# Decode attention and gated MLP on one core: output weights in 4 KB rows, down products that write output rows, and keys taken with step eight

## The chip, the cores and the metric

The kernel runs on one core of one Trainium2 chip. Its engines work in parallel, each on its own stream of instructions: PE (TensorE, matrix products, with weight loads listed apart as PEld), DVE (VectorE), ACT (ScalarE), POOL (GpSimd) and SP (SyncE), which here only issues DMAs. 16 DMA engines move data between memory and the core's SBUF. The metric is the device time of one execution in microseconds (us); less is better.

## The reference

One token for each of 4 sequences passes through a pre-norm attention block with a cache, and then a gated MLP. Inputs are bfloat16: 32 heads of 128, 8192 cached keys per head, width 512, hidden width 1792.

```python
def _A_ref(x, k_cache, v_cache, wq, wo):
    B, Sq, D = x.shape
    H, Dh = 32, 128
    q = (lambda x, *d: x.transpose(*d))((x @ wq).reshape(B, Sq, H, Dh), 0, 2, 1, 3)
    scores = jnp.einsum("bhqd,bhkd->bhqk", q, k_cache) * (Dh ** -0.5)
    p = _softmax(scores, axis=-1)
    o = jnp.einsum("bhqk,bhkd->bhqd", p, v_cache)
    return (lambda x, *d: x.transpose(*d))(o, 0, 2, 1, 3).reshape(B, Sq, H * Dh) @ wo

def _B_ref(x, w_gate, w_up, w_down):
    g = jnp.einsum("bsd,df->bsf", x, w_gate)
    u = jnp.einsum("bsd,df->bsf", x, w_up)
    h = _sigmoid(g) * u
    return jnp.einsum("bsf,fd->bsd", h, w_down)

x = A_x
h = x + _A_ref(_layernorm(x, axis=-1), A_k_cache, A_v_cache, A_wq, A_wo)
h2 = h + _B_ref(_layernorm(h, axis=-1), B_w_gate, B_w_up, B_w_down)
```

The two caches hold 256 MiB each, so nearly all of the traffic is cache. wq and wo have 4 MiB each, gate, up and down 1.75 MiB each.

## The kernel before, in words

**Pairs and slots.** The unit of work is a pair: two heads of one sequence, 4 MiB of K or of V. There are 64 K pairs and 64 V pairs. A pair fills one of four slots of `KV`: the 128 partitions are 2 heads x 64, and each partition holds 128 consecutive keys of 128 numbers, so one partition is one run of 32 KB in memory. Four pairs (the four sequences of two heads) form a group; there are 16 groups.

**Queue.** All loads are issued by SP in a fixed order (`order`, from L320): wq; K pairs 0 and 1; wo; then K and V pairs alternating, with K four pairs ahead of V; at the end the weights gate, up and down, which use slots too. Each load waits on SP until its slot is free: after the last transpose of a K pair (L367) or after the last PV product of a V pair (L458). What stands behind a waiting load on SP waits as well. K pair 0 comes in four loads, V pair 63 in two, down in three pieces (8, 4 and 2 of the 14 blocks of 128 hidden rows); every other load is one DMA. wo takes the place of wq in `Wreg`, so its load (L318) waits for the q projection (L511).

**Scores.** A K pair is worked through in 8 chunks of 16 keys per partition. DVE transposes a chunk in 32x32 blocks of 32-bit words (L367) from the slot into `kTc`, and PE multiplies it with four shifted windows of q (L386), adding the rows of all chunks and pairs of a group in one PSUM bank. Before the change, chunk s is the run of keys 16s to 16s+15 of every partition.

**Softmax.** At the end of a group come a maximum (L398, L403, L407, L411, L416), the exponential into `E_sb` (L421), the sums (L427, L429), a scaling (L430) and two transposes into `PT` (L439). These steps are spread over the following ticks, a tick being one chunk of K or V.

**PV.** Chunk m of a V pair is four products with 32 stationary columns each, which run side by side on PE (L458); their 512 moving columns are four keys that lie 16 apart.

**Selection and projection.** At the end of a group ACT copies the sums to `O_sb` (L486). Two ticks later four float32 products with `O_sb` as the stationary side pick the wanted diagonal parts and turn them (L494), DVE casts the eight columns to `OT` (L499), and two ticks after that 8 products with wo (L476) and an addition into `sth` (L481) follow. In `sth`, width lies across the partitions: column 4b+c holds block c of sequence b.

**End.** After the last group: layer norm (L205 to L223), gate and up products with the weights stationary (L582), sigmoid on ACT (L587), its product with up into `hhT` (L589), 56 down products with w_down stationary and 4 moving columns (L597) in three parts that wait for the three pieces, addition of `sth` (L602), a product that turns the result into 16 rows (L604), a cast (L606) and the store (L607).

Of the kernel before, what the change touches and what calls it, by code (L numbers as in the profile page):

```python
# [5 lines left out]
BF16 = mybir.dt.bfloat16  # L6
FP32 = mybir.dt.float32
# [8 lines left out]
GH = 8  # L16
# [63 lines left out]
def bass_sequential_preLN__mha_block_cached__glu_gated_glu__decode_kernel(  # L80
# [32 lines left out]
    with ExitStack() as es:  # L113
        def SB(name, shape, dt):
            return es.enter_context(nc.sbuf_tensor(name, shape, dt))
# [13 lines left out]
        xnT = SB("xnT", [128, NDC * B], BF16)  # L129
        hnT = SB("hnT", [128, NDC * B], BF16)  # L130
        q_all = SB("q_all", [128, NH], BF16)
        selrep = SB("selrep", [128, 4, 128], BF16)
        amask = SB("amask", [128, 4], BF16)
        q2 = SB("q2", [128, 4, NH], BF16)
        Lq = SB("Lq", [128, NLQ, 4, W], BF16)
        KV = SB("KV", [128, NSL, R * 128], BF16)
        kTc = SB("kTc", [128, NKT, RC * 64], FP32)
        E_sb = SB("E_sb", [128, 512], BF16)
        PT = SB("PT", [128, 2, PTW], BF16)
        mpart = SB("mpart", [128, 1], FP32)  # L140
        mrow = SB("mrow", [1, GH], FP32)
# [1 line left out]
        sig = SB("sig", [128, 1], FP32)  # L143
        rsum = SB("rsum", [128, 1], FP32)
        O_sb = SB("O_sb", [128, 512], FP32)
        OT = SB("OT", [128, 2, GH], BF16)
        sg_sb = SB("sg_sb", [128, NFT * B], FP32)
        hhT = SB("hhT", [128, NFT * B], BF16)
        h2T = SB("h2T", [128, NDC * B], BF16)
        o_sb = SB("o_sb", [NDC * B, 128], BF16)  # L150
        dummy = SB("dumm", [128, 2], FP32)
        WREG = H * D
        Wreg = SB("Wreg", [128, WREG], BF16)
        wq_v = Wreg[:, :].rearrange("p (c f) -> p c f", c=NDC)
        wo_v = Wreg[:, :].rearrange("p (h f) -> p h f", h=H)

        def raw(t):
            return t.tensor if hasattr(t, "tensor") else t
# [19 lines left out]
        keys += [f"sl{i}" for i in range(NSL)] + [f"k0p{i}" for i in range(4)] + [f"vl{i}" for i in range(2)]  # L178
        for k in keys:
            prog.sems[k] = es.enter_context(nc.semaphore("s_" + k))  # L180

# [45 lines left out]
        def f_xT(e):  # L227
# [19 lines left out]
            bass.AP(raw(M8), 0, [[GH, 128], [GP, 2], [0, 16], [1, GP]])), [t_m8])  # L247


        t_am = emit("dve", lambda e: e.tensor_reduce(  # L250
            amask[:, :], identf[:, :].rearrange("p (a j) -> p a j", a=4), AX.X, ALU.max), [t_identf])
        for c in range(2):
# [61 lines left out]
        t_qproj = []  # L314

        def emit_wo():
            src = A_wo.rearrange("(h p) f -> p h f", p=128)
            t_wo.append(prog.dma("sp", "wo", lambda e: e.dma_start(wo_v[:, :, :], src), [t_qproj[0]]))  # L318

        steps = [("k", n) for n in range(LAGP)]  # L320
        for n in range(NP):
# [13 lines left out]
        def pump():  # L335
            while next_dma[0] < len(order) and ready(*order[next_dma[0]]):
                kind, n = order[next_dma[0]]
                next_dma[0] += 1
                if kind == "k":
                    emit_pair("k", n, A_k_cache, t_k, "k0p", 4 if n == 0 else 1)  # L340
                elif kind == "v":
                    emit_pair("v", n, A_v_cache, t_v, "vl", 2 if n == NP - 1 else 1)
                elif kind == "wq":
                    emit_wq()
                elif kind == "wo":
                    emit_wo()
                else:
                    emit_weight(kind)
# [7 lines left out]
        t_oev = {}  # L356
        t_ptc = {}
        t_pvg = {}
        st_ = dict(xs=t_xst, xo=None, lq=None, h=t_h, ot=[None, None])
        t_lq = {}  # L360

        KVW = KV[:, :, :].bitcast(FP32)

        def transposes(n, s):
            u = NCH * n + s
            slot = slot_of["k", n]
            t_copy[u] = emit("dve", lambda e: e.transpose(  # L367
                kTc[:, u % NKT, :], KVW[:, slot, 64 * RC * s:64 * RC * (s + 1)]), [t_k[n][s * len(t_k[n]) // NCH], t_score.get(u - NKT)])
            if s == NCH - 1:
                t_tr[n] = t_copy[u]  # L370

# [70 lines left out]
        def pv(u):  # L442
            n, m = u // NCH, u % NCH
            g, i = n // GP, n % GP
            first = i == 0 and m == 0
            last = i == GP - 1 and m == NCH - 1
            slot = slot_of["v", n]
            half = m // 4
            w = [t_v[n][half * len(t_v[n]) // 2], t_ptc[g]]
            if first and g > 1:  # L450
                w.append(t_oev[g - 2])

            def f(e):
                mms = []
                for j in range(4):
                    rr = 4 * (m % 4) + j
                    o = (2 * rr + half) * 128 + i * 32
                    mms.append(e.matmul(obank(g)[32 * j:32 * (j + 1), :], PT[:, g % 2, o:o + 32],  # L458
                                        in_slot(slot, [[RC * 128, 4], [1, 128]], (64 * half + rr) * 128),
                                        start=first, stop=last, tile_position=(0, 32 * j)))  # L460
                return mms if last else mms[-1]
            tok = emit("pe", f, w, incs=4 if last else 1)
            if m == NCH - 1:
                t_pv[n] = tok
            if last:
                t_pvg[g] = tok

        def project(g, t_ot):
            ob = g % 2

            def f(e):
                ins = None
                for c in range(NDC):
                    for hh in range(2):
                        h = 2 * g + hh
                        ins = e.matmul(cols(bank[XO][:, 64:64 + NDC * B], c), wo_v[:, h, 128 * c:128 * (c + 1)],  # L476
                                       OT[:, ob, B * hh:B * (hh + 1)], start=(hh == 0), stop=(hh == 1))
                return ins
            t = emit("pe", f, [t_ot, *t_wo])
            st_["ot"][ob] = t  # L480
            st_["h"] = st_["xo"] = emit("dve", lambda e: e.tensor_tensor(  # L481
                sth[:, 0:NDC * B], sth[:, 0:NDC * B], bank[XO][:, 64:64 + NDC * B], ALU.add), [t, st_["h"]])

        def finish(g):
            ob = g % 2
            t_oev[g] = emit("act", lambda e: e.activation(O_sb[:, :], obank(g), ACT.Copy),  # L486
                            [t_pvg[g], st_.get("sel")])
            box = {}
# [100 lines left out]
        t_hh = emit("dve", lambda e: e.tensor_tensor(hhT[:, :], sg_sb[:, :], bank[UBK][:, 0:NF], ALU.mult), [t_sg, t_u])  # L589

        wd_v, t_wd = t_w["wd"]
        for i in range(len(WDT) - 1):
            def f_down(e, i=i):
                ins = None
                for t in range(WDT[i], WDT[i + 1]):
                    for c in range(NDC):
                        ins = e.matmul(cols(bank[DBK], c), wd_v[:, t, 128 * c:128 * (c + 1)],  # L597
                                       hhT[:, B * t:B * (t + 1)], start=(t == 0 and c == 0),
                                       stop=(t == NFT - 1), skip_group_check=True)
                return ins  # L600
            t_d = emit("pe", f_down, [t_hh, t_wd[i]])
        t_h2 = emit("dve", lambda e: e.tensor_tensor(  # L602
            h2T[:, :], sth[:, 0:NDC * B], bank[DBK][:, 0:NDC * B], ALU.add), [t_d, st_["h"]])
        t_o = emit("pe", lambda e: e.matmul(bank[XS][0:NDC * B, 0:128], h2T[:, :], ident[:, :],  # L604
                                            start=True, stop=True), [t_h2])
        t_oc = emit("dve", lambda e: e.tensor_copy(o_sb[:, :], bank[XS][0:NDC * B, 0:128]), [t_o])  # L606
# [58 lines left out]
```

## Time and profile before

| | |
|---|---|
| median of 3 runs | 1295.3 us (1295.19 to 1295.32) |
| profiled execution, its own time | 1295.28 us |
| its span | 1293.4 us |
| PE busy | 800.3 us (62%) |
| DVE busy | 720.8 us (56%), of which the transposes L367 587.7 us, x512 |
| ACT, POOL busy | 28.0 us, 10.3 us |
| moved by DMA | 551.45 MB, mean 426 GB/s over the span |

The span is what the profiler records between the first and the last instruction; 1.88 us of the execution's time lie outside it. Busy shares are means over the whole span. The profile also cuts the span into 40 slices of 32.3 us, and gives the busy tenths of each engine and the rate of the DMAs for each. "The chain" is found by going back from the last instruction to what released it, and so on to the start. In the listing of DMA issues, the time to landing counts from the issue on SP, so it includes the wait behind earlier loads of the same queue.

### The profile page before, as it was taken

What the parts mean: (1) busy time and instruction counts of PE and PEld (TensorE: products, weight loads), DVE (VectorE), ACT (ScalarE), POOL (GpSimd) and SP (SyncE); (2) the same over time, 40 slices, a digit from 0 to 9 for tenths busy, and PEclk for the clock granted to TensorE, in tenths of its full rate; (3) what the DMA queues carried; (4) which work ended last, traced back from release to release, by engine and by line L of the source; (5) the groups of instructions that cost most, each with busy time, mean ns of one, the idle gap of its engine ahead of it and who ended that gap; (6) DMA issues with size and microseconds to landing.
All of it is one profiled execution on the core that took longest, in us unless ns stands there. A gap on an engine that the chain in (4) does not pass through costs nothing.

```text
span 1293.4 us, 10558 instructions
## 1 busy us (share of the span) xinstructions
PE 800.3 (62%) x4761; PEld 318.5 (25%) x4761; DVE 720.8 (56%) x766; ACT 28.0 (2%) x56; POOL 10.3 (1%) x11
## 2 busy tenths in 40 slices
PE   4576556647558566566656667576575666566464
PEld 2122222213223122222222223122222222222122
DVE  5585655637555455545647556465555646556340
ACT  0000000000000000000000000000000000000001
POOL 3000000000000000000000000000000000000000
PEclk9698788777787787787786887787887887877775
DMA  9999999999999999999999999999999999999997
GB/s 394 408 429 435 427 433 432 427 434 430 430 431 430 433 429 432 429 433 429 429 436 429 429 433 427 435 428 430 435 426 434 428 433 434 424 435 431 428 432 306
DMA packets 26244, 551.45 MB, mean 426 GB/s; under 512 B 2260, under 2 KB 8152, under 8 KB 9176
## 3 DMA queue, kind: packets, MB, share of 16 engines
q1 hardware_dynamic: 26192, 550.78, 99.5%
q8 instruction: 37, 0.61, 0.2%
q14 instruction: 7, 0.06, 0.0%
q10 hardware_dynamic: 8, 0.00, 0.0%
HBM read 550.77 MB, written 0.00 MB: 426 GB/s over the span
## 4 chain that ended last, share of the span: by engine, by line
DMA 76%; DVE 22%; SPq 1%; PE 1%; issue 0%
DMA KV<-in_A_k_cache_dram 72%; DVE kTc L367 22%; DMA KV<-in_A_v_cache_dram 2%; DMA Wreg<-in_A_wq_dram 1%; SPq L302 1%; DMA KV<-in_B_w_down_dram 1%; PE PS L458 0%; PE PS L511 0%; PE PS L597 0%; SPq L318 0%; PE PS L604 0%; DVE o_sb L606 0%; DVE h2T L602 0%
## 5 line engine op out<-in xcount | busy, mean ns | idle before, releaser
L386 PE MATMUL PS<-kTc,Lq 128*128 128x512 bf16 x2048 | 618.8, 462 | 429.7 <-DVE kTc L367 425.0
L367 DVE STREAM_TRANSPOSE kTc<-KV 128x1024 f32<-128x1024 f32 x512 | 587.7, 1211 | 346.2 <-DMA KV<-in_A_k_cache_dram 345.7
L386 PEld LDWEIGHTS PS<-kTc,Lq 128*128 128x128 bf16 x2048 | 215.7, 113 | 809.5 <-DVE kTc L367 539.5
L458 PE MATMUL PS<-KV,PT 128*32 128x512 bf16 x2048 | 139.5, 400 | 22.6 <-DMA KV<-in_A_v_cache_dram 13.7
L439 DVE STREAM_TRANSPOSE PT<-E_sb 64x512 bf16<-64x512 bf16 x32 | 78.4, 2450 | 1.0
L458 PEld LDWEIGHTS PS<-KV,PT 128*32 128x32 bf16 x2048 | 50.0, 99 | 85.1 <-DMA KV<-in_A_v_cache_dram 28.3
L535 DVE TENSOR_TENSOR Lq<-q,amask 128x16 bf16<-128x16 bf16 x64 | 14.2, 229 | 85.9 <-PE PS L386 85.9
L499 DVE CAST OT<-PS 128x8 bf16<-128x8 f32 x16 | 2.7, 167 | 65.2 <-PE PS L494 65.2
L421 ACT ACTIVATE E_sb<-PS,negmb 128x512 bf16<-128x512 f32 x16 | 11.0, 687 | 1195.5 <-DVE negmb L419 1195.5
L494 PEld LDWEIGHTS PS<-selq,O_sb 128*128 128x128 f32 x128 | 30.7, 332 | 7.4 <-issue 4.4
L494 PE MATMUL PS<-selq,O_sb 128*128 128x8 f32 x128 | 27.7, 345 | 0.8 <-ACT O_sb L486 0.8
L403 PE MATMUL PS<-identf,mpart 128*1 128x128 f32 x32 | 6.1, 271 | 13.8 <-DVE mpart L398 13.8
L429 DVE RECIPROCAL rsum<-PS 128x1 f32<-128x1 f32 x16 | 2.7, 169 | 19.4 <-PE PS L427 19.3
L481 DVE TENSOR_TENSOR sth<-sth,PS 128x16 f32<-128x16 f32 x16 | 2.7, 171 | 18.0 <-PE PS L476 18.0
L398 DVE TENSOR_REDUCE mpart<-PS 128x1 f32<-128x512 f32 x16 | 10.9, 684 | 1.7 <-PE PS L386 1.7
L486 ACT ACTIVATE O_sb<-PS 128x512 f32<-128x512 f32 x16 | 9.6, 597 | 54.9 <-PE PS L458 54.9
L476 PEld LDWEIGHTS PS<-OT,Wreg 128*128 128x128 bf16 x128 | 6.9, 113 | 9.1 <-issue 7.9
L511 PE MATMUL PS<-xnT,Wreg 128*128 128x4 bf16 x128 | 3.6, 166 | 8.9 <-DMA Wreg<-in_A_wq_dram 8.9
L427 PE MATMUL PS<-sig,Gmat 128*128 128x1 f32 x32 | 6.0, 257 | 4.5 <-ACT E_sb L421 4.5
L407 DVE TENSOR_REDUCE mrow<-PS 1x8 f32<-1x128 f32 x16 | 4.4, 276 | 7.1 <-PE PS L458 7.1
L427 PEld LDWEIGHTS PS<-sig,Gmat 128*128 128x128 f32 x32 | 4.8, 187 | 12.1 <-ACT E_sb L421 11.9
L416 PE MATMUL PS<-identf,rowpad 128*128 128x1 f32 x32 | 6.0, 257 | 2.8 <-DVE rowpad L411 2.8
(65 smaller groups left out, 82.5 us busy)
## 6 DMA issues: line engine op xcount, KB each, us to landing
KV<-in_A_k_cache_dram SPq DMA_DIRECT2D x63, 4096.0 KB, 29.7
KV<-in_A_v_cache_dram SPq DMA_DIRECT2D x63, 4096.0 KB, 34.5
Wreg<-in_A_wq_dram SPq DMA_DIRECT2D x1, 4096.0 KB, 12.6
KV<-in_A_k_cache_dram SPq DMA_DIRECT2D x4, 1024.0 KB, 18.1
Wreg<-in_A_wo_dram SPq DMA_DIRECT2D x1, 4096.0 KB, 29.0
KV<-in_A_v_cache_dram SPq DMA_DIRECT2D x2, 2048.0 KB, 30.9
KV<-in_B_w_gate_dram SPq DMA_DIRECT2D x1, 1792.0 KB, 27.2
KV<-in_B_w_up_dram SPq DMA_DIRECT2D x1, 1792.0 KB, 24.9
```

What stands on the lines that cost most here:

```text
L302: t_w[kind] = (wd_v, [prog.dma("sp", f"wd{i}", lambda e, i=i: e.dma_start(wd_v[:, WDT[i]:WDT[i + 1], :], src[:, WDT[i]:WDT[i + 1], :]), w) ...
L367: t_copy[u] = emit("dve", lambda e: e.transpose(kTc[:, u % NKT, :], KVW[:, slot, 64 * RC * s:64 * RC * (s + 1)]), [t_k[n][s * len(t_k[n]) ...
L386: ins = e.matmul(sbank(g), Lq[:, n % NLQ, ce, off:off + 128], k3[:, :, ce // 2, :, ce % 2], start=first and ce == 0, stop=last and ce == 3)
L398: t_mx = emit("dve", lambda e: e.tensor_reduce(mpart[:, :], sbank(g), AX.X, ALU.max), [t_score[GP * NCH * (g + 1) - 1], st_.get("p1")])
L421: box["a2"] = emit("act", lambda e: e.activation(E_sb[:, :], sbank(g), ACT.Exp, bias=negmb[:, 0:1], scale=SCALE, accum_out=sig[:, 0:1]), [ ...
L427: t = emit("pe", lambda e: e.matmul(bank[XS][:, 130:131], Gmat[:, :], sig[:, 0:1], start=True, stop=True), [box["a2"], t_gm])
L439: t_ptc[g] = emit("dve", lambda e, z=z, dst=dst: e.transpose(dst, E_sb[64 * z:64 * z + 64, :]), w)
L458: mms.append(e.matmul(obank(g)[32 * j:32 * (j + 1), :], PT[:, g % 2, o:o + 32], in_slot(slot, [[RC * 128, 4], [1, 128]], (64 * half + rr) ...
L476: ins = e.matmul(cols(bank[XO][:, 64:64 + NDC * B], c), wo_v[:, h, 128 * c:128 * (c + 1)], OT[:, ob, B * hh:B * (hh + 1)], start=(hh == 0) ...
L486: t_oev[g] = emit("act", lambda e: e.activation(O_sb[:, :], obank(g), ACT.Copy), [t_pvg[g], st_.get("sel")])
L494: ins = e.matmul(bank[XO][:, 0:GH], O_sb[:, 128 * q:128 * (q + 1)], bass.AP(raw(selq), q, [[32, 128], [4, 2], [8, GP]]), start=(q == 0), s ...
L535: t_lq[n] = emit("dve", lambda e: e.tensor_tensor(dst, src, keep, ALU.mult), [st_["q"], t_lq0, t_am, t_score.get(NCH * (n - NLQ + 1) - 1)])
```

## The change

1. **wo's layout.** The load of wo takes four consecutive rows of the matrix to one partition: 1024 runs of 4 KB instead of 4096 runs of 1 KB. Row 512g + 4p + e of wo then lies on partition p, so the attention output has to be brought to the matching place.
2. **Selection, turned round.** The selecting matrix (`pick`, built in the setup) is now the stationary side and `O_sb` moves, so that the result is rows of O, 64 per group; an even and an odd group share the 128 rows. After an odd group DVE casts them to `O_row` and transposes 32x32 blocks with step four into `OT`; 16 products for both groups follow, and one addition into `sth`.
3. **Step eight.** For every pair but the first, chunk s of K is the keys s, s+8, s+16 and so on of a partition. The order of the scores then makes PV chunk m use keys 16m to 16m+15, four neighbours to a product. V pair 63 comes in four loads.
4. **Down products.** The hidden vector is stationary (32 columns, of which four at step eight are not zero) and w_down moves, so that the sums are rows of the output, block c on partitions 32c to 32c+31. Four products with `res`, a zero-padded copy of `sth`, and an identity start the sums. The separate addition and the turning product go; the cast covers 128 partitions, and the store picks every eighth.
5. **Room.** `selrep` uses the space of `E_sb`, and `hhT` and `res` that of `kTc`; the latter two are zeroed by POOL after the last scores.

```diff
@@
-        selrep = SB("selrep", [128, 4, 128], BF16)
+        selrep = E_sb[:, :].rearrange("p (e j) -> p e j", e=4)
-        OT = SB("OT", [128, 2, GH], BF16)
+        pick = SB("pick", [128, 4, 64], FP32)
+        O_row = SB("O_row", [128, 128], BF16)
+        OT = SB("OT", [128, 4, 32], BF16)
-        hhT = SB("hhT", [128, NFT * B], BF16)
-        h2T = SB("h2T", [128, NDC * B], BF16)
-        o_sb = SB("o_sb", [NDC * B, 128], BF16)
+        hhT = kTc[:, 0, 0:16 * NFT].bitcast(BF16).rearrange("p (t m) -> p t m", m=32)
+        res = kTc[:, 0, 256:256 + 32 * NDC].rearrange("p (c m) -> p c m", m=32)
+        o_sb = SB("o_sb", [128, 128], BF16)
-        wo_v = Wreg[:, :].rearrange("p (h f) -> p h f", h=H)
+        wo_v = Wreg[:, :].rearrange("p (g e f) -> p g e f", g=NG // 2, e=4)
...
+        t_pk0 = emit("dve", lambda e: e.memset(pick[:, :, :], 0.0))
+        for hh in range(2):
+            t_pk = emit("dve", lambda e, hh=hh: e.tensor_copy(
+                pick[:, :, 32 * hh:32 * hh + B],
+                bass.AP(raw(selq), 4 * hh, [[32, 128], [1, 4], [8, B]])), [t_sel, t_pk0])
...
         def emit_wo():
-            src = A_wo.rearrange("(h p) f -> p h f", p=128)
-            t_wo.append(prog.dma("sp", "wo", lambda e: e.dma_start(wo_v[:, :, :], src), [t_qproj[0]]))
+            src = A_wo.rearrange("(g p e) f -> p g (e f)", p=128, e=4)
+            dst = Wreg[:, :].rearrange("p (g f) -> p g f", g=NG // 2)
+            t_wo.append(prog.dma("sp", "wo", lambda e: e.dma_start(dst, src), [t_qproj[0]]))
...
-                    emit_pair("v", n, A_v_cache, t_v, "vl", 2 if n == NP - 1 else 1)
+                    emit_pair("v", n, A_v_cache, t_v, "vl", 4 if n == NP - 1 else 1)
...
+        def chunk(n, slot, s):
+            if n == 0:
+                return KVW[:, slot, 64 * RC * s:64 * RC * (s + 1)]
+            return KVW[:, slot, :].rearrange("p (r g w) -> p r g w", g=NCH, w=64)[:, :, s, :]
...
             t_copy[u] = emit("dve", lambda e: e.transpose(
-                kTc[:, u % NKT, :], KVW[:, slot, 64 * RC * s:64 * RC * (s + 1)]), [t_k[n][s * len(t_k[n]) // NCH], t_score.get(u - NKT)])
+                kTc[:, u % NKT, :], chunk(n, slot, s)), [t_k[n][s * len(t_k[n]) // NCH], t_score.get(u - NKT)])
...
-            half = m // 4
-            w = [t_v[n][half * len(t_v[n]) // 2], t_ptc[g]]
+            w = [t_v[n][m * len(t_v[n]) // NCH], t_ptc[g]]
...
-                    rr = 4 * (m % 4) + j
-                    o = (2 * rr + half) * 128 + i * 32
-                    mms.append(e.matmul(obank(g)[32 * j:32 * (j + 1), :], PT[:, g % 2, o:o + 32],
-                                        in_slot(slot, [[RC * 128, 4], [1, 128]], (64 * half + rr) * 128),
+                    k = 4 * m + j
+                    o = k * 128 + i * 32
+                    at = [[RC * 128, 4], [1, 128]], (64 * (k % 2) + k // 2) * 128
+                    if n:
+                        at = [[1, 512]], 512 * k
+                    mms.append(e.matmul(obank(g)[32 * j:32 * (j + 1), :], PT[:, g % 2, o:o + 32], in_slot(slot, *at),
                                         start=first, stop=last, tile_position=(0, 32 * j)))
...
+            lo = 64 * (g % 2)
             def s1():
                 def f(e):
                     ins = None
                     for q in range(4):
-                        ins = e.matmul(bank[XO][:, 0:GH], O_sb[:, 128 * q:128 * (q + 1)],
-                                       bass.AP(raw(selq), q, [[32, 128], [4, 2], [8, GP]]), start=(q == 0), stop=(q == 3))
+                        ins = e.matmul(bank[XO][lo:lo + 64, 0:128], pick[:, q, :], O_sb[:, 128 * q:128 * (q + 1)],
+                                       start=(q == 0), stop=(q == 3), tile_position=(0, lo))
                     return ins
-                t = emit("pe", f, [t_oev[g], t_sel, st_["xo"]])
-                st_["sel"] = t
-                box["ot"] = emit("dve", lambda e: e.tensor_copy(OT[:, ob, :], bank[XO][:, 0:GH]),
-                                 [t, st_["ot"][ob]])
+                st_["sel"] = emit("pe", f, [t_oev[g], t_pk, st_["xo"]])
+                if g % 2:
+                    t = emit("dve", lambda e: e.tensor_copy(O_row[:, :], bank[XO][:, 0:128]),
+                             [st_["sel"], st_.get("tr")])
+                    st_["tr"] = emit("dve", lambda e: e.transpose(
+                        OT[:, :, :], O_row[:, :].rearrange("p (i e) -> p e i", e=4)), [t, st_.get("ot")])
+                    st_["xo"] = t
             def s2():
-                project(g, box["ot"])
-            return [(2, s1), (4, s2)]
+                def f(e):
+                    ins = None
+                    for c in range(NDC):
+                        for k in range(4):
+                            ins = e.matmul(cols(bank[XO][:, 128:128 + NDC * B], c),
+                                           wo_v[:, g // 2, k, 128 * c:128 * (c + 1)], OT[:, k, 0:B],
+                                           start=(k == 0), stop=(k == 3))
+                    return ins
+                st_["ot"] = t = emit("pe", f, [st_["tr"], st_["xo"], *t_wo])
...
+            return [(2, s1), (4, s2)] if g % 2 else [(2, s1)]
...
+        t_hh0 = emit("pool", lambda e: e.memset(hhT[:, :, :], 0.0), [t_score[NCH * NP - 1]])
+        t_rs0 = emit("pool", lambda e: e.memset(res[:, :, :], 0.0), [t_score[NCH * NP - 1]])
...
+        t_res = emit("dve", lambda e: e.tensor_copy(
+            res[:, :, 0:25:8], sth[:, 0:NDC * B].rearrange("p (b c) -> p c b", b=B)), [st_["h"], t_rs0])
         t_hn, _ = layernorm(sth, st_["h"], 1, hnT, bank[XS], st_["xs"])
...
+        def rows(c):
+            return bank[DBK][32 * c:32 * (c + 1), 0:128]
+        def f_res(e):
+            ins = None
+            for c in range(NDC):
+                ins = e.matmul(rows(c), res[:, c, :], identf[:, :], start=True, stop=False,
+                               tile_position=(0, 32 * c), skip_group_check=True)
+            return ins
+        t_r = emit("pe", f_res, [t_res])
...
-                        ins = e.matmul(cols(bank[DBK], c), wd_v[:, t, 128 * c:128 * (c + 1)],
-                                       hhT[:, B * t:B * (t + 1)], start=(t == 0 and c == 0),
-                                       stop=(t == NFT - 1), skip_group_check=True)
-                return ins
-            t_d = emit("pe", f_down, [t_hh, t_wd[i]])
-        t_h2 = emit("dve", lambda e: e.tensor_tensor(
-            h2T[:, :], sth[:, 0:NDC * B], bank[DBK][:, 0:NDC * B], ALU.add), [t_d, st_["h"]])
-        t_o = emit("pe", lambda e: e.matmul(bank[XS][0:NDC * B, 0:128], h2T[:, :], ident[:, :],
-                                            start=True, stop=True), [t_h2])
-        t_oc = emit("dve", lambda e: e.tensor_copy(o_sb[:, :], bank[XS][0:NDC * B, 0:128]), [t_o])
+                        mms.append(e.matmul(rows(c), hhT[:, t, :], wd_v[:, t, 128 * c:128 * (c + 1)],
+                                            start=False, stop=(t == NFT - 1), tile_position=(0, 32 * c),
+                                            skip_group_check=True))
+                return mms[-4:]
+            t_d = emit("pe", f_down, [t_hh, t_wd[i], t_r], incs=4)
+        t_oc = emit("dve", lambda e: e.tensor_copy(o_sb[:, :], bank[DBK][:, 0:128]), [t_d])
         t_out = prog.dma("sp", "out", lambda e: e.dma_start(
-            out.rearrange("b s (c p) -> (b s c) p", p=128), o_sb[:, :]), [t_oc])
+            out.rearrange("b s (c p) -> c (b s) p", p=128),
+            bass.AP(raw(o_sb), 0, [[8 * 128, NDC * B], [1, 128]])), [t_oc])
```

More of the change, by code (lines that the diff above doesn't have):

```diff
@@ L177, in bass_sequential_preLN__mha_block_cached__glu_gated_glu__decode_kernel @@
         keys = ["sp", "act", "dve", "pool", "pe", "x", "out", "wg", "wu", "wd0", "wd1", "wd2", "wq", "wo"]
-        keys += [f"sl{i}" for i in range(NSL)] + [f"k0p{i}" for i in range(4)] + [f"vl{i}" for i in range(2)]
+        keys += [f"sl{i}" for i in range(NSL)] + [f"k0p{i}" for i in range(4)] + [f"vl{i}" for i in range(4)]
         for k in keys:
@@ L358, in bass_sequential_preLN__mha_block_cached__glu_gated_glu__decode_kernel @@
         t_pvg = {}
-        st_ = dict(xs=t_xst, xo=None, lq=None, h=t_h, ot=[None, None])
+        st_ = dict(xs=t_xst, xo=None, lq=None, h=t_h)
         t_lq = {}
         KVW = KV[:, :, :].bitcast(FP32)
+        def chunk(n, slot, s):
+            if n == 0:
+                return KVW[:, slot, 64 * RC * s:64 * RC * (s + 1)]
+            return KVW[:, slot, :].rearrange("p (r g w) -> p r g w", g=NCH, w=64)[:, :, s, :]
         def transposes(n, s):
@@ L466, in pv @@
                 t_pvg[g] = tok
[L468 to L477, printed above, removed]
-                return ins
[L479 to L482, printed above, removed]
         def finish(g):
-            ob = g % 2
             t_oev[g] = emit("act", lambda e: e.activation(O_sb[:, :], obank(g), ACT.Copy),
                             [t_pvg[g], st_.get("sel")])
-            box = {}
+            lo = 64 * (g % 2)
             def s1():
@@ L493, in f @@
                     for q in range(4):
-                        ins = e.matmul(bank[XO][:, 0:GH], O_sb[:, 128 * q:128 * (q + 1)],
-                                       bass.AP(raw(selq), q, [[32, 128], [4, 2], [8, GP]]), start=(q == 0), stop=(q == 3))
-                    return ins
-                t = emit("pe", f, [t_oev[g], t_sel, st_["xo"]])
-                st_["sel"] = t
-                box["ot"] = emit("dve", lambda e: e.tensor_copy(OT[:, ob, :], bank[XO][:, 0:GH]),
-                                 [t, st_["ot"][ob]])
-            def s2():
-                project(g, box["ot"])
-            return [(2, s1), (4, s2)]
+                        ins = e.matmul(bank[XO][lo:lo + 64, 0:128], pick[:, q, :], O_sb[:, 128 * q:128 * (q + 1)],
+                                       start=(q == 0), stop=(q == 3), tile_position=(0, lo))
+                    return ins
+                st_["sel"] = emit("pe", f, [t_oev[g], t_pk, st_["xo"]])
[5 more added lines that the diff above has]
+                    st_["xo"] = t
+            def s2():
+                def f(e):
[7 more added lines that the diff above has]
+                st_["ot"] = t = emit("pe", f, [st_["tr"], st_["xo"], *t_wo])
+                st_["h"] = st_["xo"] = emit("dve", lambda e: e.tensor_tensor(
+                    sth[:, 0:NDC * B], sth[:, 0:NDC * B], bank[XO][:, 128:128 + NDC * B], ALU.add), [t, st_["h"]])
+            return [(2, s1), (4, s2)] if g % 2 else [(2, s1)]
         def q_projection():
@@ L588, in bass_sequential_preLN__mha_block_cached__glu_gated_glu__decode_kernel @@
         t_u = emit("pe", glu_mm(t_w["wu"][0], bank[UBK]), [t_hn, t_w["wu"][1]])
-        t_hh = emit("dve", lambda e: e.tensor_tensor(hhT[:, :], sg_sb[:, :], bank[UBK][:, 0:NF], ALU.mult), [t_sg, t_u])
+        t_hh = emit("dve", lambda e: e.tensor_tensor(
+            hhT[:, :, 0:25:8], sg_sb[:, :].rearrange("p (t b) -> p t b", b=B),
+            bank[UBK][:, 0:NF].rearrange("p (t b) -> p t b", b=B), ALU.mult), [t_sg, t_u, t_hh0])
         wd_v, t_wd = t_w["wd"]
+        def rows(c):
+            return bank[DBK][32 * c:32 * (c + 1), 0:128]
@@ L592, in bass_sequential_preLN__mha_block_cached__glu_gated_glu__decode_kernel @@
+        def f_res(e):
[5 more added lines that the diff above has]
+        t_r = emit("pe", f_res, [t_res])
         for i in range(len(WDT) - 1):
             def f_down(e, i=i):
-                ins = None
+                mms = []
                 for t in range(WDT[i], WDT[i + 1]):
@@ L596, in f_down @@
                     for c in range(NDC):
-                        ins = e.matmul(cols(bank[DBK], c), wd_v[:, t, 128 * c:128 * (c + 1)],
-                                       hhT[:, B * t:B * (t + 1)], start=(t == 0 and c == 0),
-                                       stop=(t == NFT - 1), skip_group_check=True)
-                return ins
-            t_d = emit("pe", f_down, [t_hh, t_wd[i]])
-        t_h2 = emit("dve", lambda e: e.tensor_tensor(
-            h2T[:, :], sth[:, 0:NDC * B], bank[DBK][:, 0:NDC * B], ALU.add), [t_d, st_["h"]])
```

## The prediction

> **What bounds the kernel now.** I read the page first: engines, slices, chain.
>
> ```profile
> PE 800.3 (62%) x4761; PEld 318.5 (25%) x4761; DVE 720.8 (56%) x766; ACT 28.0 (2%) x56; POOL 10.3 (1%) x11
> DMA  9999999999999999999999999999999999999997
> GB/s 394 408 429 435 427 433 432 427 434 430 430 431 430 433 429 432 429 433 429 429 436 429 429 433 427 435 428 430 435 426 434 428 433 434 424 435 431 428 432 306
> DMA 76%; DVE 22%; SPq 1%; PE 1%; issue 0%
> ```
>
> No compute engine is above 62%, while the DMA engines are full in 39 of 40 slices at about 431 GB/s. The chain's 22% on DVE must not be read as DVE being the bound: a cache load is issued when the transposes have emptied its slot, and at that moment other loads are still queued. So time is bytes over rate, plus a start and a tail. Only three slices are low: the first two and the last. I therefore asked for the windows around wo, the first of them ending where wq lands (columns: stretch, length, busy time of PE, PEld, DVE, ACT, POOL, clock, DMA share, GB/s).
>
> ```profile
> 13.30:34.00 20.70, 13.73 (x164) 7.40 (x164) 10.71 (x16) 0.00 (x0) 0.00 (x0) 0.95 1.01 419
> 34.00:46.00 12.00, 8.93 (x32) 3.33 (x32) 9.33 (x9) 0.00 (x0) 0.00 (x0) 0.79 1.11 375
> 46.00:55.70 9.70, 0.00 (x0) 0.00 (x0) 0.00 (x0) 0.00 (x0) 0.00 (x0) 0.66 1.00 432
> 55.70:94.57 38.87, 28.12 (x114) 9.89 (x118) 34.34 (x36) 0.78 (x2) 0.00 (x0) 0.90 1.00 431
> ```
>
> The slow stretch is the one in which wo moves, with the engines fully busy. The table of DMA issues and the start of the timeline date it (first lines: size and us to landing; then start, duration).
>
> ```profile
> Wreg<-in_A_wo_dram SPq DMA_DIRECT2D x1, 4096.0 KB, 29.0
> KV<-in_B_w_gate_dram SPq DMA_DIRECT2D x1, 1792.0 KB, 27.2
> KV<-in_B_w_up_dram SPq DMA_DIRECT2D x1, 1792.0 KB, 24.9
> ...
> 16.95 0.38 SPq L318 DMA_DIRECT2D Wreg<-in_A_wo_dram  x1
> 33.97 9.13 DVE L367 STREAM_TRANSPOSE kTc<-KV 128x1024 f32<-128x1024 f32 x8 [3.84 <-DMA KV<-in_A_k_cache_dram]
> ```
>
> K pair 1, queued ahead of wo, lands at 33.95; wo lands at 16.95 + 29.0 = 45.95; K pair 2, behind it, at 55.69. So 4 MB of wo took 12.0 us where K pair 2 took 9.74. Last, the end of the chain:
>
> ```profile
> 1270.63 11.50 SPq L302
> 1282.12 0.04 issue
> 1282.17 8.15 DMA KV<-in_B_w_down_dram
> 1290.32 0.05 issue
> 1290.37 0.39 PE PS L597 x8
> 1290.76 0.02 issue
> 1290.78 0.18 DVE h2T L602
> 1290.96 0.04 issue
> 1291.00 0.29 PE PS L604
> 1291.30 0.02 issue
> 1291.32 0.28 DVE o_sb L606
> ```
>
> The last piece of w_down, not arithmetic, sets the end: hhT is written by 1287.67 (L589: 1287.46 + 0.21), and the three down pieces then start at 1288.33, 1289.67 and 1290.37 as they land.
>
> **The change part by part**, against the profiled execution: 1295.28 us, 1.88 us of it outside the 1293.4 us span. It lies 0.02 us below the median of 1295.3.
>
> *wo in 4 KB rows.* The same 4 MB goes in 1024 runs instead of 4096. Bounds: no gain (12.0 us, the 1 KB rows) and the full rate of the 32 KB cache rows (four pairs per 38.84 us of chain, one per 9.71): a gain of 2.3. The nearest rows are the gate and up weights, in 3.5 KB runs. The last V piece lands at 1276.40, gate at 1253.60 + 27.2 = 1280.8, up at 1260.48 + 24.9 = 1285.4: 4.4 and 4.6 us for 1792 KB, or 10.1 and 10.5 us scaled to 4096 KB. I take the mean, 10.25: a gain of 1.75 us. It should survive to the end, since every later load stands behind wo in a queue that never empties. One K issue after wo now holds SP for 22.5 us of a 23.62 us stretch; that wait should shrink, but it has only ever delayed loads that would have queued anyway: 0.
>
> The Trainium skill, "DMA: Bandwidth & Descriptors", Specifications, puts the smallest transfer for line rate at 512 B. By it 1 KB rows already run at full rate, this part gains nothing and the total would be 1294.8. The 375 GB/s stretch contradicts it here, and I go by the stretch.
>
> *Last V pair in four loads of 8 KB rows, not two of 16 KB.* Two issues more on SP, about 0.4 us each (0.80 for two now), at 1242.8; the next issue there, gate, waits for a slot until 1253.60, so they cost nothing. Rate: the two halves landed 4.9 us apart (1271.47, 1276.40) against 4.86 for half a 32 KB-row pair, so shorter rows cost between 0 and 0.2. I take 0.1.
>
> *Keys with step eight.* All but the first 8 of 512 transposes read 16 runs of 64 words, 2 KB apart, instead of one run; the PV products read 512 columns in one run. The trace has no such read. Bounds for the transpose: 1.2 us as now (the inner run is still 64 words) and the rate of L439, which scatters every element 80 B apart: 2450 ns for 512, 4.8 ns each, so 4.9 us. I take 1.2, as two whole 32-word blocks still lie side by side in each run. The Trainium skill, "SBUF — State Buffer", Door 1, says that strides cost where accesses leave a 16-byte line; 256 B runs use every line fully. No run here shows that yet. PV gains or loses nothing visible: L458 is beside the DMA.
>
> *Selection and projection.* Per group, four selections of 128x64 against 128 columns; per two groups a cast, a transpose and 16 products. Until the last group this lies beside DMA: DVE is 56% busy and PE 62%, and a few us in all vanish there. At the end it lies between the last V landing (1276.40) and hhT (1287.67). Steps: last PV products 8 instead of 16, 1.90 to 0.95 (-0.95); selection 1.88 now, 8 passes of 128 columns then, between 8 x 0.107 (the 0.43 us per 512 columns of L386) and 8 x 0.27 (L403), -1.0 to +0.3; cast 0.29 (L517) for 0.17, +0.12; transpose of 128 elements at 1.2 to 4.8 ns, +0.15 to +0.61; 8 more products, +0.3 to +0.4 (L476); copy of sth into res, +0.17 (L238); residual products ahead of the down ones on PE, 0.2 to 0.86 less the 0.21 of L589 beside which they run, 0 to +0.65. Sum -1.2 to +1.3. The wait for w_down's first piece absorbs 0.66 of this and the waits for the later ones most of the rest: 0, at worst +0.5.
>
> *Setup and zeroing.* One memset and two copies more on DVE, under 1 us; DVE stands idle from 11.64 to 16.95, when q_all is due. Two small memsets on POOL after the last scores (1238), with 40 us in hand. 0.
>
> *Down products into rows.* 56 products of 32 rows by 128 columns, four side by side, replace 56 of 4 columns. L458 runs four such 32-wide products of 512 columns in 0.43 us, so 0.11 per four here; its four loads span 0.16. After the last piece: two rounds, 0.21 to 0.32 beside 0.29 now; I take +0.05. Gone: h2T (0.18), the transposing product (0.29) and their gaps, 1290.78 to 1291.32 = 0.54. The cast goes from 16 to 128 partitions at the same 128 elements (L517: 0.29 against 0.28). Output is again 16 runs of 256 B. Sum -0.5, with bounds -0.65 and +0.1.
>
> Total: 1295.28 - 1.75 + 0.1 - 0.5 = 1293.1.
>
> **Rivals.**
> 1. *Short rows weren't what made wo slow*; 4 KB rows take 12.0 us too. For: 3.5 KB gate and up rows aren't 4 KB ones, and their landings are blurred by the tail. Against: nothing else differs between that stretch and its neighbours. 1295.28 + 0.1 - 0.5 = 1294.9.
> 2. *Strided transposes become the bound* (slower). Place: L367. One K and one V pair take 19.42 us of DMA; DVE's other work per K pair is (720.8 - 587.7)/64 = 2.1 us, so DVE takes over once a transpose exceeds (19.42 - 2.1)/8 = 2.16 us. Above that each extra 0.1 us costs 0.1 x 504 = 50 us; at 2.4 us the kernel is at about 1293 + 121 = 1414. Against: runs of 64 words stay whole.
> 3. *Down products don't overlap.* 56 x 0.107 = 6.0 us from 1288.33 end at 1294.3, not 1290.76: +3.6, so about 1296.7. For: stationary and moving sides are swapped, with short moves. Against: L458 does overlap with the same 32-wide tiles.
> 4. *4 KB rows run like 32 KB ones*, and the tail saves 0.65: 1295.28 - 2.3 - 0.65 = 1292.3.
>
> **How the numbers follow.** Forecast 0.62, rivals 0.12, 0.08, 0.12 and 0.06. The prediction is the forecast's 1293.1. Its own range is 1292.3 to 1294.2 (row rate 10.0 to 10.9 us, tail up to +0.3). The range 1292.0 to 1295.3 takes in rivals 1 and 4 and the milder half of 3; outside are rival 2, the rest of 3 and a rest of 0.05, under 0.2. A measurement of this kernel can tell 0.2%, 2.6 us, from no change: under 1292.7 is faster, over 1297.9 slower. Faster: rival 4 and a third of the forecast, 0.26. Slower: rival 2 and a worse 3, 0.10. Same: 0.64.
>
> **What would show it.** wo lands about 1.75 us earlier relative to K pair 1, and K pair 2 near 54; the stretch at 375 GB/s rises above 410. The transposes stay near 1.2 us. No PE or DVE step stands between the down products and the final cast. The last w_down piece still releases the last products. I am wrong if K pair 2 still lands at 55.7, if the transposes exceed 1.5 us, or if the last w_down piece lands more than 1 us off its shifted time: its issue is held for 11.5 us on SP, and I have only one example of that.

## The result, and the profile after

The changed kernel takes 1293.49 us (median of 20 runs, 1293.25 to 1293.94) against 1295.32 us (20 runs, 1295.05 to 1295.56) for the one before: a ratio of 0.9986, interval 0.998 to 0.9993. That is 1.83 us less; the forecast was 2.15 us less. The change is smaller than 0.2%, but the two sets of runs don't overlap. The profiled span went from 1293.4 to 1291.7 us.

The windows around wo, after the change (columns as in the prediction: stretch, length, busy time of PE, PEld, DVE, ACT, POOL, clock, DMA share, GB/s):

```profile
13.30:34.00 20.70, 13.22 (x160) 7.08 (x157) 10.82 (x16) 0.00 (x0) 0.00 (x0) 1.00 1.01 426
34.00:46.00 12.00, 8.85 (x32) 3.15 (x32) 9.22 (x9) 0.00 (x0) 0.00 (x0) 0.86 1.08 441
46.00:55.70 9.70, 0.62 (x2) 0.28 (x3) 1.93 (x2) 0.00 (x0) 0.00 (x0) 0.62 1.00 432
```

The slow stretch is gone: 441 GB/s where there were 375, though this window now takes in 2 us of K pair 2 as well. wo's line among the DMA issues of the same kernel (size, us to landing), and then the start of its chain (start, duration):

```profile
Wreg<-in_A_wo_dram SPq DMA_DIRECT2D x1, 4096.0 KB, 27.4
```

```profile
16.63 0.39 SPq L326
17.02 0.04 issue
17.06 36.69 DMA KV<-in_A_k_cache_dram
53.75 0.02 issue
53.77 9.14 DVE kTc L380 x8
```

wo is issued at 16.63 and lands at 44.03, not 45.95. Counted from the landing of K pair 1 (33.84, before 33.95), wo took 10.2 us instead of 12.0. K pair 2, behind it, took 9.7 and lands at 53.75, not 55.69: 1.94 us of the change is already there after 54 us. At the last landing of V pair 63 it is 1.60 us (1276.36 before, 1274.76 now); the finer loads of that pair cost some 0.1 of the difference, and the other 0.2 lie within the spread between executions of one kernel (0.5 us). The groups of instructions show no change in the long middle (first line: the kernel before, the others after):

```profile
L367 DVE STREAM_TRANSPOSE kTc<-KV 128x1024 f32<-128x1024 f32 x512 | 587.7, 1211 | 346.2 <-DMA KV<-in_A_k_cache_dram 345.7
L380 DVE STREAM_TRANSPOSE kTc<-KV 128x1024 f32<-128x1024 f32 x512 | 586.8, 1209 | 371.2 <-DMA KV<-in_A_k_cache_dram 363.4
L473 PE MATMUL PS<-KV,PT 128*32 128x512 bf16 x2048 | 138.0, 397 | 23.2 <-DMA KV<-in_A_v_cache_dram 14.3
```

A transpose of 16 separate runs takes 1209 ns where one run took 1211. The chain at the end:

```profile
1270.69 0.90 SPq L309
1271.59 0.04 issue
1271.63 8.58 SPq L309
1280.21 0.04 issue
1280.26 8.43 DMA KV<-in_B_w_down_dram
1288.68 0.04 issue
1288.73 0.51 PE PS L624 x8
1289.24 0.02 issue
1289.26 0.29 DVE o_sb L629
```

and SP's own timeline behind it, before the change and after:

```profile
1291.63 0.37 SPq L607 DMA_DIRECT2D out_dram<-o_sb  x1
1289.58 0.69 SPq L630 DMA_DIRECT2D out_dram<-o_sb  x1
```

The last piece of w_down still sets the end, and the two steps between the products and the cast are gone. But from the landing of that piece to the end of the span 3.06 us pass (1288.68 to 1291.74), where it was 3.09 (1290.32 to 1293.41). The 0.54 us taken out came back in two places. The last products take 0.51 us instead of 0.39, so that the issue of the store starts only 0.41 us sooner after the landing (0.90 for 1.31). And the store takes 0.38 us longer: from the start of its issue to its last completion signal in the trace 1.76 us pass instead of 1.38, and the issue alone takes 0.69 instead of 0.37.

### The profile page after: what moved, and what is told of

It is laid out like the page before. It is cut to its first block, busy times and chain, and to the rows that moved or that the text cites. A ratio compares the mean times of both kernels' runs of the same rounds, so it can differ in the third digit from the quotient of the medians.

```text
span 1291.7 us, 10570 instructions
## 1 busy us (share of the span) xinstructions
PE 777.4 (60%) x4768; PEld 308.4 (24%) x4768; DVE 722.6 (56%) x761; ACT 28.0 (2%) x56; POOL 10.9 (1%) x13
## 4 chain that ended last, share of the span: by engine, by line
DMA 76%; DVE 21%; PE 1%; SPq 1%; issue 0%; ACT 0%
DMA KV<-in_A_k_cache_dram 72%; DVE kTc L380 21%; DMA KV<-in_A_v_cache_dram 2%; DMA Wreg<-in_A_wq_dram 1%; PE PS L399 1%; SPq L309 1%; DMA KV<-in_B_w_down_dram 1%; PE PS L521 0%; PE PS L473 0%; ACT E_sb L434 0%; DVE mpart L411 0%; PE PS L624 0%; PE PS L429 0%; SPq L326 0%; PE PS L440 0%
## 5 line engine op out<-in xcount | busy, mean ns | idle before, releaser
L399 PE MATMUL PS<-kTc,Lq 128*128 128x512 bf16 x2048 | 589.1, 446 | 450.7 <-DVE kTc L380 446.7
L380 DVE STREAM_TRANSPOSE kTc<-KV 128x1024 f32<-128x1024 f32 x512 | 586.8, 1209 | 371.2 <-DMA KV<-in_A_k_cache_dram 363.4
L399 PEld LDWEIGHTS PS<-kTc,Lq 128*128 128x128 bf16 x2048 | 210.0, 110 | 817.4 <-DVE kTc L380 545.9
L491 PE MATMUL PS<-O_sb,pick 128*64 128x128 f32 x128 | 31.5, 428 | 0.8 <-ACT O_sb L483 0.8
L491 PEld LDWEIGHTS PS<-O_sb,pick 128*64 128x64 f32 x128 | 25.1, 224 | 13.8 <-issue 12.2
L429 PEld LDWEIGHTS PS<-identf,rowpad 128*128 128x128 f32 x32 | 4.8, 187 | 10.4 <-DVE rowpad L424 10.3
```

Source lines behind the costliest of these rows:

```text
L380: t_copy[u] = emit("dve", lambda e: e.transpose(kTc[:, u % NKT, :], chunk(n, slot, s)), [t_k[n][s * len(t_k[n]) // NCH], t_score.get(u - N ...
L399: ins = e.matmul(sbank(g), Lq[:, n % NLQ, ce, off:off + 128], k3[:, :, ce // 2, :, ce % 2], start=first and ce == 0, stop=last and ce == 3)
L429: t = emit("pe", lambda e: e.matmul(bank[XS][:, 128:129], rowpad[:, :], identf[:, 0:1], start=True, stop=True), [box["d2"], t_rp0])
L491: ins = e.matmul(bank[XO][lo:lo + 64, 0:128], pick[:, q, :], O_sb[:, 128 * q:128 * (q + 1)], start=(q == 0), stop=(q == 3), tile_position= ...
```

## The experiments

Each kernel ran beside the kernel before, which took 1295.26 to 1295.33 us in these comparisons; times are medians.

**Where the gain came from: wo by length of run.** All three edits stand in the changed kernel's `emit_wo`: 1 KB runs (one of four rows per load), 2 KB runs (two of four), and a control with 4 KB runs in four loads.

```diff
+            src = A_wo.rearrange("(g p e) f -> p g e f", p=128, e=4)
+            for j in range(4):
+                t_wo.append(prog.dma("sp", "wo", lambda e, j=j: e.dma_start(wo_v[:, :, j, :], src[:, :, j, :]), [t_qproj[0]]))
...
             src = A_wo.rearrange("(g p e) f -> p g (e f)", p=128, e=4)
+            for j in range(2):
+                t_wo.append(prog.dma("sp", "wo", lambda e, j=j: e.dma_start(
+                    dst[:, :, 1024 * j:1024 * (j + 1)], src[:, :, 1024 * j:1024 * (j + 1)]), [t_qproj[0]]))
...
+            for j in range(4):
+                t_wo.append(prog.dma("sp", "wo", lambda e, j=j: e.dma_start(
+                    dst[:, 2 * j:2 * (j + 1), :], src[:, 2 * j:2 * (j + 1), :]), [t_qproj[0]]))
```

> The changed kernel with wo loaded into the new places in runs of 1 KB (four loads of 1 MB, one per row of four), all else as changed. Row-length theory: wo takes 12.0 us again instead of 10.2, K pair 2 lands near 55.7 instead of 53.75, time about 1293.5 + 1.9 = 1295.4 us. Rival, the gain came from the other parts (keys, selection, down products): stays at 1293.5 us.

> The changed kernel with wo in runs of 2 KB (two loads of 2 MB). If every run costs a fixed time on top of its bytes: 4096 runs cost 12.0 - 9.7 = 2.3 us, so 2048 cost 1.15 and 1024 cost 0.57; wo takes 10.9 us and the time is 1294.1 us. Rival, only runs below some length are slow and 2 KB is long enough: 1293.5 us, or as slow as 1 KB: 1295.4 us.

> Control for the two others: the changed kernel with wo in runs of 4 KB, but as four loads of 1 MB. If run length alone counts: 1293.5 us, K pair 2 at 53.75. If the number of loads counts, it is slower, and the two others have to be read against this one.

| wo | K pair 2 lands | time |
|---|---|---|
| 1 KB runs, four loads | 55.65 | 1295.41 us (1295.24 to 1295.68) |
| 2 KB runs, two loads | 54.32 | 1294.10 us (1293.97 to 1294.36) |
| 4 KB runs, four loads | 53.83 | 1293.67 us (1293.35 to 1293.85) |
| 4 KB runs, one load (the changed kernel) | 53.75 | 1293.49 us |

The same stretch in the windows, first with 1 KB and then with 2 KB runs:

```profile
34.00:46.00 12.00, 9.77 (x32) 3.60 (x32) 9.34 (x9) 0.00 (x0) 0.00 (x0) 0.72 1.12 375
```

```profile
34.00:46.00 12.00, 8.93 (x32) 3.30 (x32) 9.17 (x9) 0.00 (x0) 0.00 (x0) 0.81 1.06 407
```

Putting the short runs back, with everything else changed, brings back the 375 GB/s and the old time. So the run length of this one load is the whole measurable gain. The 2 KB case falls on the line of a fixed cost per run. Against the one load of 4 KB runs it is about 1.92 us for 3072 runs more (1 KB) and 0.61 us for 1024 more (2 KB), both 0.6 ns a run over 16 engines, or some 10 ns on the engine that carries it. The number of loads counts little: the control is 0.18 us above the single load, with overlapping runs. Against this control, four loads against four, the 1 KB case is 1.74 us, 0.57 ns a run. The packets of these loads in the traces agree: at the median they last 51 ns with 1 KB, 88 with 2 KB and 164 with 4 KB, so the same 4 KB cost 12 to 13 ns more for every further packet.

**V pair 63 in two loads.**

```diff
-                    emit_pair("v", n, A_v_cache, t_v, "vl", 4 if n == NP - 1 else 1)
+                    emit_pair("v", n, A_v_cache, t_v, "vl", 2 if n == NP - 1 else 1)
```

> The changed kernel with V pair 63 in two loads of 16 KB runs instead of four of 8 KB. Theory: the shorter runs cost about 0.15 us of DMA time and nothing on the path uses the earlier products, so 1293.3 to 1293.5 us. Rival: the later last products (16 instead of 8 after the last landing, +0.9 us) reach the end through hhT, which stands only 0.4 us ahead of w_down's first piece: 1293.8 to 1294.2 us.

1293.38 us (1293.26 to 1293.48): 0.11 us less than the changed kernel, at the edge of what these runs tell. The finer pieces cost about what was priced, and the products they bring forward weren't needed earlier: in both kernels the cast starts 0.58 us after the last signal of w_down (here 1288.44 and 1289.02), so that landing still sets the end.

**Keys with step eight alone**, in the kernel before (`chunk` and the PV addresses of the diff, V pair 63 in two).

```diff
+                kTc[:, u % NKT, :], chunk(n, slot, s)), [t_k[n][s * len(t_k[n]) // NCH], t_score.get(u - NKT)])
```

> The kernel before, with the keys at step eight alone (V pair 63 still in two loads). Theory: a transpose of 16 runs of 64 words takes the same 1.2 us and PV is beside the DMA: 1295.3 us. Rival: the strided reads disturb the DMA's writes into SBUF, or free slots later, and the rate of the cache loads falls: above 1295.6 us.

1295.40 us (1295.09 to 1295.59) beside 1295.30 (1295.00 to 1295.65): no difference. Its transposes:

```profile
L372 DVE STREAM_TRANSPOSE kTc<-KV 128x1024 f32<-128x1024 f32 x512 | 587.7, 1210 | 349.4 <-DMA KV<-in_A_k_cache_dram 348.9
```

**Down products into rows alone**, in the kernel before: all that the diff has from `t_hh0` and `t_res` to the store, and the space for `hhT`, `res` and `o_sb`.

> The kernel before, with the down products into rows alone (residual products, final cast and store included). By the prediction's sum it saves 0.5 us: 1294.8 us. By the trace of the changed kernel the gain is eaten by longer last products (0.51 for 0.39 us) and a longer issue of the store (0.69 for 0.37 us): 1295.2 us.

1295.25 us (1295.13 to 1295.48) beside 1295.30: nothing to be told. Its chain at the end and SP's line show the gain and its loss side by side:

```profile
1290.64 0.04 issue
1290.69 0.51 PE PS L614 x7
1291.20 0.02 issue
1291.22 0.29 DVE o_sb L619
```

```profile
1291.54 0.70 SPq L620 DMA_DIRECT2D out_dram<-o_sb  x1
```

From the landing of w_down's last piece to the end of the cast, 0.87 us instead of 1.28, so 0.41 less; then the store's issue takes 0.33 us more.

**What makes the store's issue longer.**

```diff
-            out.rearrange("b s (c p) -> c (b s) p", p=128),
+            out.rearrange("b s (c p) -> (b s c) p", p=128),
```

> The changed kernel with the store written as 16 rows one after the other in memory, as before the change, instead of a 4 x 4 x 128 pattern; the rows of the output then come in another order (block before sequence). The source is the same 16 partitions with step eight. If the pattern in memory makes the store's issue take 0.69 us instead of 0.37: issue 0.37 us, 1293.2 us. Rival, the step of eight partitions does: issue 0.69 us, 1293.5 us.

```profile
1289.65 0.58 SPq L630 DMA_DIRECT2D out_dram<-o_sb  x1
```

1293.57 us (1293.43 to 1293.94). Neither expectation for the issue held. Issues were 0.37 us from 16 neighbouring partitions, 0.58 from partitions eight apart to rows in order, and 0.69 with the 4 x 4 x 128 pattern in memory as well. The partition step therefore goes with the larger share, 0.21 of 0.32. The 0.11 us saved on the issue didn't reach the time, and the signals say why: the last one comes 1.76 us after the issue began with either pattern in memory, and 1.38 us with the store of before. Up to its landing the store is 0.38 us longer with the partition step alone, and the pattern adds nothing to that.

**Can the same rule be used on w_down?** First in runs of 8, 4 and 2 KB:

```diff
-                src = B_w_down.rearrange("(t p) f -> p t f", p=128)
...
+                src = B_w_down.rearrange("(p t) f -> p (t f)", t=NFT)
...
-                        ins = e.matmul(bk[:, B * t:B * (t + 1)], wv[:, c, 128 * t:128 * (t + 1)],
+                        ins = e.matmul(bk[:, B * t:B * (t + 1)], wv[:, c, t:t + NFT * 127 + 1:NFT],
```

> The changed kernel with w_down taken 14 rows to a partition, so that its three pieces have runs of 8, 4 and 2 KB instead of 1 KB (384 runs instead of 1792); gate and up take their stationary columns with step 14 to match. Fixed cost per run of 0.56 ns (2.3 us for 4096): 1408 runs fewer, -0.8 us, 1292.7 us, the last w_down piece landing 0.8 us earlier. Rival A, the end is set by how long SP is held at w_down's second piece (8.6 us) and by uneven engines, and not by run length: 1293.5 us. Rival B, weight loads with step 14 slow the 112 gate and up products, which have 0.4 us of room: 1293.5 us or more, with gate and up taking clearly more than 3.15 us.

1296.24 us (1296.10 to 1296.53), 2.75 us slower than the changed kernel. The timeline of the products that load gate and up with step 14:

```profile
1282.82 6.89 PE L597 MATMUL PS<-hnT,KV 128*128 128x4 bf16 x112 [1.31 <-DVE hnT L225]
```

It is rival B: 6.89 us instead of 3.15, 61 ns for each load and product instead of 28. w_down's last piece landed 0.4 us earlier (1288.3), half of the 0.8 that was expected, and why only half was not tried; but now PE set the end. So the rows were taken in pairs only, which makes the step two:

```diff
+                src = B_w_down.rearrange("(a p e) f -> p a (e f)", p=128, e=2)
...
+                        ins = e.matmul(bk[:, B * t:B * (t + 1)], wv[:, c, 256 * (t // 2) + t % 2:256 * (t // 2) + t % 2 + 255:2],
```

> The changed kernel with V pair 63 in two loads and w_down in runs of 2 KB: two neighbouring rows to a partition, 896 runs instead of 1792; gate and up take stationary columns with step two. By the cost per run measured with wo (0.56 to 0.6 ns each over 16 engines): 896 runs fewer, -0.5 us, and -0.1 for V pair 63: 1292.9 us, if weight loads with step two are as quick as packed ones (3.15 us for gate and up). If they are slow like those with step 14 (6.9 us): 1295 us or more.

1293.21 us (1293.05 to 1293.53). Its timeline:

```profile
1283.11 3.15 PE L598 MATMUL PS<-hnT,KV 128*128 128x4 bf16 x112 [1.31 <-DVE hnT L225]
...
1287.02 1.69 PE L626 MATMUL PS<-KV,kTc 128*32 128x128 bf16 x56 [0.18 <-PE PS L617]
```

Step two costs nothing. All 56 down products now run without a stop from 1287.02 and end at 1288.7, while the last piece of w_down landed at 1288.0: what they wait for now is the work ahead of them on PE and hhT, no longer the DMA. The same with V pair 63 in four loads again:

> The kernel of wd_pairs with V pair 63 in four loads again, as in the changed kernel. In wd_pairs the last w_down piece landed at 1288.0 but the down products ended at 1288.8, because hhT came late: 16 PV products stood between the last V landing and the rest. With 8 there, 0.9 us less, the down products should end half a us after the last piece again. Theory: about -0.25 us, 1292.95 us. Rival, the shorter runs of V pair 63 cost as much as the earlier products gain: 1293.2 us.

1293.15 us (1292.90 to 1293.52). The last piece (1288.2) sets the end once more, and the time is that of its sister within the spread: here the rival held. Both are about 0.3 us faster than the changed kernel and 2.1 us faster than the one before, and are the best complete kernels of this study.

The Trainium skill, "SBUF — State Buffer", Door 1, says that steps are free as long as a 16-byte line is hit at least twice. The two weight loads agree: step two of 2-byte numbers stays in the line and took 28 ns, step 14 (28 B) leaves it each time and took 61. No step between the two was measured.

**Why the end is ragged.** Windows of the changed kernel from 1276 us on (columns as above):

```profile
1276.00:1278.00 2.00, 1.37 (x7) 1.37 (x8) 0.00 (x0) 1.97 (x3) 0.00 (x0) 0.50 1.06 384
1278.00:1280.00 2.00, 1.19 (x19) 0.70 (x17) 0.65 (x3) 0.09 (x1) 0.00 (x0) 0.50 0.66 247
1280.00:1282.00 2.00, 0.60 (x2) 0.50 (x2) 1.14 (x8) 0.08 (x1) 0.00 (x0) 0.50 0.77 257
```

From 1278 us on, ten microseconds before the last byte, the DMA engines are no longer full, but for one stretch (1282 to 1284 us, share 1.00). The trace has the times of a load's completion signals: 16 for each load, read here as one from each DMA engine. Of the changed kernel, in us:

```
load                   first seven signals   other nine
wq                     12.4 to 12.7          12.8 to 13.0
K pair 0, 3rd piece    19.9 to 20.2          20.2 to 20.4, one at 21.6
V pair 63, last piece  1266.6 to 1267.3      1272.9 to 1274.8
w_down, last piece     1283.8 to 1284.6      1286.9 to 1288.7
```

Seven signals come at one time, nine up to 8.2 us later. The distance grows in steps of over 1 us, one signal at a time. The first step falls together with the first 16 KB packet of the instruction queue (at 18.1 us, 1.03 us long). The later ones do too. Add up, for each load from wq to the last piece of V pair 63, how far the nine late signals lie behind the mean of the first seven. From one load to the next this sum grows by 1.2 to 2.5 us (mean 1.6) each of the 35 times that such a packet lies between, and by 0.03 us on average (at most 0.9) the 100 times that none does. That made a theory to test, by dropping instructions:

```diff
+            if 0 < m < NCH - 1:
+                return
             tok = emit("pe", f, w, incs=4 if last else 1)
```

> The changed kernel without three quarters of the PV products (chunks 1 to 6 of every V pair are left out, so the output isn't the reference's); every load stays. It tests what makes the DMA engines end apart: at the end, 7 of a load's 16 completion signals come 6 to 8 us before the other 9, and the gap grows in steps of about 1.2 us, one engine at a time, at about the times of the 16 KB instruction packets (35 of them). Instruction-fetch theory: 1536 products, with their weight loads 3072 instructions of 64 B (0.67 MB for 10570), are 12 packets fewer; each of the nine engines is then late by one or two steps less, so the gap at the last V landing falls from 8.2 us to about 6 and the time by 1.2 to 2.5 us, to 1291.0 to 1292.3 us. Rival, those packets cost only their bytes, spread over all engines: 0.2 MB at 431 GB/s, 1293.0 us. Rival, the engines drift apart for another reason: 1293.5 us with the gap at 8.

1291.64 us (1291.41 to 1291.87), inside the range of the first theory. The DMA queues of the page, first the changed kernel and then this one (packets, MB, share):

```profile
q8 instruction: 37, 0.61, 0.2%
```

```profile
q8 instruction: 25, 0.41, 0.1%
```

12 packets fewer, and the last piece of V pair 63 signals at 1266.7 to 1267.5 and 1269.9 to 1272.8: the early seven where they were, the late nine 2 to 3 us earlier, the distance 6.1 us instead of 8.2. Fewer bytes for all engines would have moved all sixteen. This run alone leaves a rival, since the products that were left out also read `KV` and `PT`, and the granted clock was 0.75 instead of 0.79; the steps at the packets in the changed kernel don't depend on it.

**Giving the early engines more.**

```diff
+                    done[n].append(prog.dma("sp", "vl3", lambda e: e.dma_start(
+                        KV[0:119, slot, q * s:q * (s + 1)], src[0:119, q * s:q * (s + 1)]), w))
+                    t_vx.append(prog.dma("sp", "vl4", lambda e: e.dma_start(
+                        KV[119:128, slot, q * s:q * (s + 1)], src[119:128, q * s:q * (s + 1)]), w))
...
```

> The changed kernel with the last quarter of V pair 63 loaded as 119 partitions and 9 partitions. The Trainium skill, DMA: Bandwidth & Descriptors, Why a DMA increments its semaphore by 16 and not by 1, says that a load uses the largest number of engines up to 16 that divides its slowest dimension, the lowest-numbered ones: 7 engines for 119 partitions, 9 for 9. No run here has shown that yet. If these 7 are the 7 early ones: the 9 late engines lose 2.3 us of work, the V landing comes 2.2 us earlier, the last w_down piece too, 1291.3 us. If they are among the late ones: 17 partitions on each instead of 8 add 2.7 us, 1296 us. If the number of engines does not depend on the partitions: 1293.5 us.

1305.4 us (1304.89 to 1306.29), worse than any of the expectations. The two loads left 7 and 9 late signals, besides one each at the issue, as the same section of the Trainium skill says ("DMA: Bandwidth & Descriptors", Why a DMA increments its semaphore by 16 and not by 1). The seven came at 1273.9 to 1275.8 (four) and 1284.8 to 1287.3 (three), so this set mixes early and late engines and the idea falls. The quarter before had signalled by 1278.1 at the latest, so 17 runs of 8 KB took about 9 us on an engine, where 8 of them take 2.5, little more than half the speed. They weren't alone in this: packets of 8 KB last 314 ns on average up to 1262 us and 615 between 1268 and 1274, those of the untouched quarters among them, and the core's DMA rate from 1265 to 1275 us is 213 to 236 GB/s, where the changed kernel has 408 to 413. Why was not tried.

## Why the prediction was right, point by point

- **wo in 4 KB rows, -1.75 us.** Right, a little small, and the whole of the gain: -1.92 us by putting the short runs back (-1.74 against the control), -1.94 at the landing of K pair 2. wo took 10.2 us where 10.25 was taken, so the gate and up rows were a good nearest row. Rival 1 (12.0 us) and rival 4 (9.7) are out. The gain was carried to the end, as the argument of the queue that never empties said. The 512 B of the prediction, which spoke against it, do not describe this load.
- **V pair 63 in four, +0.1.** +0.11 by undoing it, at the edge of what the runs tell.
- **Keys with step eight, 0.** Right: 1209 and 1210 ns for 1211, and the same time alone. Rival 2 is out.
- **Selection and projection, 0 (bounds -1.2 to +1.3).** From the last V landing to hhT 11.27 us became 11.45 (1274.81 to 1286.26). Inside it, last PV products -0.9, selection +0.1, cast and transpose together +0.5 (the transpose 0.31, between its bounds), projection +0.2, copy +0.1, and one step that the sum had not seen: L603 writes hhT with step eight and takes 0.40 us for 0.21. As argued, the wait for w_down absorbed it: the first piece landed at 1286.56, 0.3 us after hhT.
- **Down products into rows, -0.5. This term was mis-sized: alone it gave 0.05 us, which the runs can't tell from nothing.** The two removed steps went as predicted, and the products overlap (rival 3 is out). Two of its steps failed. "Output is again 16 runs of 256 B" was taken to mean an unchanged store; its issue went from 0.37 to 0.69 us, on the path, and the time from the start of its issue to its landing grew by 0.38 us. And the last products were put at 0.29 us now, where the prediction's own line of the chain has 0.39, and at +0.05; they took 0.51, +0.12.
- **The last piece of w_down.** It landed 1.64 us earlier, where -1.75 and +0.1 give 1.65.

The sum was -2.15 and -1.83 was measured. The parts measured singly give -1.92 + 0.11 - 0.05 = -1.86. So the down products were taken some 0.45 us too large and wo some 0.17 too small. That the two errors partly cancel is luck, but the range didn't need it. Two slips in the prediction bear on nothing: the total by the 512 B is 1294.9, as in rival 1, when the 0.1 for V pair 63 is counted, and rows at 10.0 us with the best tail end at 1292.6, so the 1292.3 of its own range is that of rival 4.

## What to carry to other kernels

In a kernel whose DMA queue never empties, count the runs as well as the bytes: each cost about 0.6 ns of the queue's time here, measured with runs of 1, 2 and 4 KB, and that one load gave the whole gain of a change in five parts. A removed step at the end counts only after the steps that its new layout lengthens (a strided write, a store from spread partitions) are priced too, the issue and the landing of a DMA among them. And before longer runs are bought with strided weight columns, look at the step: two was free, fourteen doubled the time of 112 loads.

## What the runs showed of the hardware that was not expected

The kernel's own instruction stream competes with its data. 37 packets of the instruction queue, each of 16 KB and 1.02 to 1.13 us long, delay only nine of the 16 DMA engines, judging by the signals: at the last V landing nine were 6 to 8 us behind the other seven, which were done with their last share at 1284.6 us, 4 us before the last of the nine. Each packet adds about 1.6 us to the delay of the nine taken together. Dropping 3072 of 10570 instructions, and with them 12 packets, saved 1.85 us although every data load stayed. The signals and that run agree on it; which nine engines these are, and why always nine, remains open, and so does what an even spread would save. So an instruction hidden behind the DMAs isn't quite free: here about 0.6 us per thousand.
